# Row sums of the first six head pairs: two pairs per product group on four 32-column strips of TensorE, and all key-weight absolute values on VectorE

## The chip, the cores and the metric

The program runs on one core of one Trainium2 chip. The metric is the device time of one execution, in microseconds. The engines are TensorE (PE in the profile; its weight loads are PEld), VectorE (DVE), ScalarE (ACT), GpSimd (POOL) and SyncE (SP, which here only issues DMAs).

## What is computed

Soft-capped attention feeds an RWKV-like channel mix. Sizes: batch 8, 12 heads, 448 positions, head size 64, model width 768, inner width 1024.

```
scores = cap * tanh(scale * q @ k.T / cap)
attn   = exp(scores - max);  attn /= sum(attn) + 1e-09
x      = attn @ v                          # heads side by side: [8, 448, 768]
xk, xr = mixes of x with the x of the position before (mu_k, mu_r)
k      = relu(xk @ w_k);  v = k * k @ w_v;  r = sigmoid(xr @ w_r)
out    = r * v
```

w_k, w_v and w_r arrive as 64-bit floats, in two 32-bit words, and are rebuilt on the chip.

## The kernel before, in words

The work goes by **pairs of heads**: 48 pairs, six per batch entry. A pair's exponentials stand transposed, keys on partitions. The 448 keys make three groups of 128 and 64 left over; the left keys of two pairs (an even one and the one behind it) share one tile, `p_left`, with one pair's on partitions 0 to 63 and the other's on 64 to 127.

A program that is written out in **steps** sets the order on every engine: each step runs through a list of operation names (`START_EVEN` and `START_ODD` for steps 0 to 13, lines 77 to 83) and emits each operation's instructions. Every engine works through its own queue strictly in that order. In `step` (line 794) the dictionary `pair` says how far behind the step an operation's pair is: S, tanh and exp work on pair i in step i, V (`values`) on pair i-1, and `sum_recip`, `norm`, `mix_old`, `mix_new` on pair i-2. VL (`values_left`) and L (`scores_left`) stand in even steps only and serve two pairs each.

The operations that matter here, one by one:

- **S0, S1, S2** (`scores`, line 267): two products per key group, one per head, f32, into a PSUM tile `s`. **L** (line 278): four products of 64 rows and 64 columns, the left keys of two pairs. All these use the pool `ps_s`, which has **two** tiles: a score tile can be written when the `tanh` that reads the tile two before it is done.
- **tanh and exp** (lines 288, 294): each one ACT instruction of 128x896; the result is a tile `p`. In an even step ACT's list reads tanh0, exp0, tanh1, tanhL, expL, exp1, mix_old, tanh2, exp2; in an odd one tanh0, exp0, mix_old, tanh2, tanh1, exp1, exp2.
- **V** (line 303): six products of 64 columns, two heads side by side, into PSUM tile `pv`. **VL** (line 313): four products of 64x64 that add the left keys of two pairs.
- **O** (`ones`, line 324), for the pairs in `ONES`, 0 to 5, only: products of a constant 1/32 with the tiles `p`, whose output has the row sums 64 times over. A pair takes six products of 64 columns, two side by side. **OL** (`ones_left`, line 334): four of 64x64 for the left keys of two pairs. O stands in each step from 1 to 6 (pair i-1), OL at the head of steps 2, 4 and 6.
- **sum_recip** (line 343): on DVE, a transposing reduction of the sums, the guard `grd` added, a reciprocal and a transposition that spreads it. **norm** multiplies the values by it; **mix_old** (ACT, line 409) and **mix_new** (DVE, line 419) make the mixed row from it and free `pv`.
- For pairs 6 and on the sums are made by DVE reductions (`red`, line 354) and a round trip through DRAM.
- **K** (`kpart`, line 448): products of the key matrix, in fp32r, that begin in step 7. Their tiles come from the pool `ps_k`, also that of the row sums.
- **Weights**: `weight_load` brings a piece of 128x384; `weight_abs` (line 511) takes the absolute value of the upper words; five DVE instructions per piece follow, one per `f` (`fill`) or in `weight_rest`. Pieces 0 to 15 are of w_k. `DABS` (line 42) names the pieces whose absolute value is on DVE: 0 and 1; ACT does the others.

Of the kernel before, what the change touches and what calls it, by code (L numbers as in the profile page):

```python
# [9 lines left out]
F32 = mybir.dt.float32  # L10
F32R = mybir.dt.float32r
AF = mybir.ActivationFunctionType
ALU = mybir.AluOpType
# [3 lines left out]
B, H, S, D = 8, 12, 448, 64  # L17
NP = H // 2
DM = H * D
DF = 1024  # L20
NF = DF // 128
ND = DM // 128
# [3 lines left out]
P = 128  # L26
# [12 lines left out]
QA = QM + KL  # L39
NSTEP = NPAIR + 6  # L40
ONES = (0, 1, 2, 3, 4, 5)
DABS = (0, 1)
Q2 = 1
PS = 10
PACE = 0.85
# [23 lines left out]
HALF = (slice(0, 64), slice(64, 128))  # L69
NB = 2 * S // 32  # L70
# [3 lines left out]

START_EVEN = """more weight_load gather load_qk load_v weight_store load_vl OL f sum_recip weight_low weight_rest S0 K S1 V
VL L relu tanh0 exp0 tanh1 k_store tanhL expL qk_high weight_sum f recip norm f red0 f S2 K exp1 relu mix_old
qk_low redL mix_new red1 x_high x_low k_store tanh2 K O K relu exp2 k_store f red2 weight_abs rec_store
x_store rec_load"""  # L80
START_ODD = """load_qk weight_load gather load_v sum_recip f f norm f f K S0 tanh0 exp0 mix_old relu k_store O K S1 S2 tanh2
tanh1 relu exp1 k_store exp2 V f weight_low red0 recip mix_new weight_rest weight_sum x_high qk_high qk_low
x_low K K weight_abs relu red1 red2 k_store x_store rec_store weight_store more rec_load"""
UNIT = """gather f f recip load_v.0 weight_load S0.0 S1.0 S2.0 V.0 V.1 S0.1 S1.1 S2.1 VL L tanh1.0 tanh0.0 exp0.0
# [9 lines left out]
def order(i):  # L94
    ops = LAST if i == NPAIR else UNIT if SW <= i <= NPAIR + 1 else START_ODD if i % 2 else START_EVEN
    if i == 8:
        ops = ops.replace("tanh2 K O K relu exp2", "K O K relu tanh2 exp2")
# [15 lines left out]
class Body:  # L113
# [209 lines left out]

    def ones(self, i):

        if i not in self.SUM:
            self.SUM[i] = self.ps_k.tile([P, 512], F32, name="kps")
        for g in range(3):
            ph = self.P32[i, g]
            for h, p in enumerate(HALF):  # L330
                self.nc.tensor.matmul(self.SUM[i][p, 0:S], self.one, ph[:, h, :],  # L331
                                      start=(i % 2 == 0 and g == 0), stop=(i % 2 == 1 and g == 2))

    def ones_left(self, i):

        ph = self.P32[i, "L"]
        self.SUM[i + 1] = self.ps_k.tile([P, 512], F32, name="kps")
        for p in range(2):
            for h, o in enumerate(HALF):
                self.nc.tensor.matmul(self.SUM[i + p][o, 0:S], self.one[HALF[p]], ph[HALF[p], h, :],  # L340
                                      start=(p == 1), stop=(p == 0))

    def sum_recip(self, i):

        nc = self.nc
        t = self.up.tile([P, NB // 2], F32, name="se", bufs=1)
        nc.vector.tensor_reduce(out=t, in_=self.SUM.pop(i)[:, 0:S].rearrange("p (b k) -> p b k", k=32),
                                axis=mybir.AxisListType.X, op=ALU.add, apply_transpose=True)
        nc.vector.tensor_scalar(t, t, self.grd, None, op0=ALU.add)
        nc.vector.reciprocal(t, t)  # L350
        r = self.R[i] = self.up.tile([P, 2, S], F32, name="r", bufs=1)[:, 0]
        nc.vector.transpose(out=r, in_=t.unsqueeze(2).to_broadcast([P, NB // 2, 32]))
# [441 lines left out]
    def step(self, i):  # L794

        even, unit = i % 2 == 0, SW <= i <= NPAIR + 1
        if unit and not even:
            return
        if self.maxima and even and i < NPAIR:
            self.row_maxima(i)  # L800
            self.row_maxima(i + 1)
        pair = dict(load_qk=i + 3, qk_high=i + 2, qk_low=i + 2, load_v=i, S=i, tanh=i, exp=i, red=i, load_vl=i, L=i)
        pair.update(dict.fromkeys("V gather recip rec_store rec_load".split(), i - 1))
        pair.update(O=i - 1, OL=i - 2)
        pair.update(dict.fromkeys("sum_recip norm mix_old mix_new x_high x_low x_store VL".split(), i - 2))
        name = dict(S="scores", V="values", VL="values_left", L="scores_left", O="ones", OL="ones_left")
        late = "gather recip rec_store rec_load red".split()
        first = "O OL sum_recip".split()
        two = "gather recip rec_store rec_load".split()
        nk = 0  # L810
        if unit:
            pair.update(VL=i - 2)
        seen = {}
        for op in order(i):
            g, j1 = (), 0
            if len(op) == 2 and op[0] in "lpdcs":
                self.tail_work(op)
                continue
            if "." in op:
                op, j1 = op[:-2], int(op[-1])  # L820
            if op[-1] in "012L" and op not in ("L", "VL", "OL"):
                op, g = op[:-1], (op[-1] if op[-1] == "L" else int(op[-1]),)
            if op in pair:
                j = pair[op] + j1
                if unit and op == "V":
                    j -= 1
                    if j < SW - 1:
                        continue
                if op in two:
                    if unit:  # L830
                        if j - 1 < NPAIR:
                            getattr(self, op + "_two")(j - 1)
                        continue
                    if j >= SW - 2:
                        continue
                if op == "load_qk" and i == 0 and Q2:
                    self.load_qk(2)
                if 0 <= j < NPAIR and op not in (late if j in ONES else first) and not (uncut(j) and op in ('qk_high', 'qk_low')):
                    getattr(self, name.get(op, op))(j, *g)
            elif op == "next":  # L840
                self.open_first()
            elif op == "K":
                self.kpart(*self.ksplit.pop((i, nk), (0, 0)))
                nk += 1
            elif op == "f":
                if i <= NPAIR:
                    self.fill()
            elif op == "weight_load":
                self.weight_load(i + seen.get(op, 0))
                seen[op] = 1  # L850
            elif op == "more":
                for _ in range(MORE.count(i)):
                    self.weight_load(i)
# [204 lines left out]
```

## Time and profile before

| | us |
|---|---|
| median of 3 runs | 895.08 (894.81 to 895.83) |
| the profiled execution's own time | 895.82 |
| its span, first to last instruction | 894.0 |
| PE busy | 881.2 (99%) |
| DVE busy | 734.8 (82%) |
| ACT busy | 623.1 (70%) |
| POOL busy | 415.0 (46%) |

The page gives busy time per engine, the span in 40 slices, and groups of instructions. The mean granted clock of TensorE is 0.998 of 2.4 GHz. Matmuls overlap in the records, and an f32 product appears as two MATMUL records, so the pace of PE is read from the distance between the starts of neighbours, not from a record's duration. In the timeline a record's fields are its start, its length with equal neighbours merged, engine, line, operation, output and inputs, shapes, count, and, in brackets, the engine's idle time before it and what ended that.

### The profile page before, as it was taken

The numbers are of one execution on the slowest core, as the hardware profiler recorded it, in microseconds if no ns is written. First come the engines' busy times: TensorE is split into PE (matmuls) and PEld (weight loads), VectorE is DVE, ScalarE is ACT, GpSimd is POOL, SyncE is SP. The second block draws the span as 40 slices with busy tenths as digits, with TensorE's granted clock in tenths as the row PEclk, the third lists the DMA queues.
The fourth block names the chain that finished last, engine by engine and source line by source line (L and its number), as shares of the span: only waits on it lengthen the run. The fifth ranks groups of instructions, "written<-read, shape, count | busy, mean of one in ns | idle before, by whom it ended". The sixth has DMA issues, their size and how long they took to land.

```text
span 894.0 us, 14329 instructions
## 1 busy us (share of the span) xinstructions
PE 881.2 (99%) x5046; PEld 694.7 (78%) x5046; DVE 734.8 (82%) x1115; ACT 623.1 (70%) x962; POOL 415.0 (46%) x399
## 2 busy tenths in 40 slices
PE   7999999999999999999999999999999999999997
PEld 2335556767766677777676999999999999999996
DVE  5868996888987887897886789888888888888883
ACT  7898878888887787787876776655545555555451
POOL 2343354555566585676774003444345434443440
PEclk9999999999999999999999999999999999999999
DMA  7354655766656776677647963233233322332301
GB/s 261 118 167 144 207 185 163 227 193 192 193 184 193 210 224 214 201 216 243 200 148 247 330 237 95 76 110 118 79 114 110 118 87 85 119 110 83 119 28 49
DMA packets 97562, 142.97 MB, mean 160 GB/s; under 512 B 11592, under 2 KB 86984, under 8 KB 96840
## 3 DMA queue, kind: packets, MB, share of 16 engines
q1 hardware_dynamic: 89704, 129.56, 46.3%
q10 hardware_dynamic: 7776, 12.39, 3.7%
q8 instruction: 42, 0.69, 0.3%
q14 instruction: 40, 0.33, 0.1%
HBM read 94.18 MB, written 45.33 MB: 156 GB/s over the span
## 4 chain that ended last, share of the span: by engine, by line
PE 94%; ACT 3%; DVE 1%; DMA 1%; issue 0%; SPq 0%; DVEq 0%; ACTq 0%
PE kps L469 26%; PE ps2a L720 22%; PE pv L310 12%; PE ps2c L720 11%; PE s L275 11%; PE ps2b L720 5%; PE pv L319 2%; PE s L285 2%; PE kps L331 1%; ACT p L291 1%; ACT p L301 1%; DMA sq<-r 0%; DVE ro L708 0%; PE kps L340 0%; DMA w<-wk 0%
## 5 line engine op out<-in xcount | busy, mean ns | idle before, releaser
L291 ACT ACTIVATE p<-s,scl_t 128x896 f32<-128x896 f32 x144 | 139.4, 997 | 17.0 <-PE s L275 11.3
L301 ACT ACTIVATE p<-p,cap_t 128x896 f32<-128x896 f32 x144 | 145.2, 1036 | 1.9
L469 PE MATMUL kps<-xkh,wkl 128*128 128x448 f32 x384 | 143.5, 374 | 0.1
L469 PE MATMUL kps<-xkl,wkh 128*128 128x448 f32 x384 | 140.7, 366 | 0.0
L356 DVE TRANSPOSE_TENSOR_REDUCE r<-p 128x28 f32<-128x896 f32 x126 | 136.0, 1092 | 5.7 <-ACT p L301 5.4
L469 PE MATMUL kps<-xkh,wkh 128*128 128x448 f32 x384 | 140.3, 365 | 0.0
L310 PE MATMUL pv<-p,rv 128*64 128x448 f32 x576 | 115.1, 544 | 0.0
L469 PEld LDWEIGHTS kps<-xkh,wkl 128*128 128x128 f32 x384 | 72.1, 188 | 25.7 <-issue 12.3
L310 PEld LDWEIGHTS pv<-p,rv 128*64 128x64 f32 x576 | 38.6, 136 | 66.5 <-issue 57.4
L469 PEld LDWEIGHTS kps<-xkl,wkh 128*128 128x128 f32 x384 | 72.1, 188 | 8.0 <-issue 2.8
L469 PEld LDWEIGHTS kps<-xkh,wkh 128*128 128x128 f32 x384 | 72.1, 188 | 5.8
L708 DVE TENSOR_TENSOR ro<-t,ro 128x384 fp32r<-128x384 f32 x70 | 52.8, 756 | 23.2 <-ACT ro L131 23.2
L137 POOL TENSOR_TENSOR qkl<-rqk,qkh 128x832 fp32r<-128x832 f32 x34 | 67.6, 1988 | 2.7
L708 DVE TENSOR_TENSOR vo<-x,vo 128x512 fp32r<-128x512 f32 x63 | 56.3, 902 | 11.3 <-ACT vo L131 11.0
L407 DVE TENSOR_TENSOR x<-pv,r 128x448 f32<-128x448 f32 x48 | 28.1, 618 | 45.3 <-DMA r<-rec_d 43.6
L554 POOL TENSOR_TENSOR wsq<-wa,wsq 128x384 f32<-128x384 f32 x24 | 25.9, 1080 | 84.4 <-DVE wsq L545 84.4
L752 ACT ACTIVATE rs<-rs 128x384 f32<-128x384 f32 x28 | 14.7, 525 | 65.1 <-DVE rs L725 65.1
L131 ACT CAST ro<-t 128x384 fp32r<-128x384 f32 x70 | 34.3, 509 | 30.5 <-POOL t L137 30.2
L137 POOL TENSOR_TENSOR xkl<-xk,xkh 128x448 fp32r<-128x448 f32 x46 | 53.0, 1152 | 3.8
L672 DVE SCALAR_TENSOR_TENSOR t<-xc,mu_r,t 128x256 f32<-128x256 f32 (+3 forms) x120 | 53.7, 500 | 0.8
L137 POOL TENSOR_TENSOR s<-s,t 128x384 f32<-128x384 f32 x13 | 13.6, 1048 | 75.0 <-DVE ro L708 75.0
L131 ACT CAST vo<-x 128x512 fp32r<-128x512 f32 x63 | 38.9, 618 | 10.3 <-POOL x L137 6.0
(209 smaller groups left out, 2386.3 us busy)
## 6 DMA issues: line engine op xcount, KB each, us to landing
rqk<-qk SPq DMA_DIRECT2D x47, 448.0 KB
k_d<-ko ACTq DMA_DIRECT2D x54, 224.0 KB
x_d<-x SPq DMA_DIRECT2D x48, 224.5 KB
out<-cp SPq DMA_DIRECT2D x56, 192.0 KB
rv<-v SPq DMA_DIRECT2D x48, 192.0 KB
r<-rec_d SPq DMA_DIRECT2D x36, 224.0 KB
kr<-k_d SPq DMA_DIRECT2D x7, 1024.0 KB
x<-k_d SPq DMA_DIRECT2D x7, 1024.0 KB
```

The costliest lines, as they stand in the source:

```text
L131: self.nc.scalar.copy(out, x)
L137: {"p": self.nc.gpsimd, "v": self.nc.vector}[e].tensor_sub(*a)
L275: nc.tensor.matmul(s[:, h, 0:S], qk[a][p, k], qk[b][p, 0:S], start=(n == 0), stop=(n == len(terms) - 1))
L291: self.nc.scalar.activation(p32, self.S.pop((i, g))[:, :, 0:S], AF.Tanh, scale=self.scl_t)
L301: self.nc.scalar.activation(p32, p32, AF.Exp, scale=1.0 if self.maxima else self.cap_t)
L310: nc.tensor.matmul(pv[p, 0:S], v[:, g, h, :], ph[:, h, :], start=(g == 0), stop=False)
L356: self.nc.vector.tensor_reduce(out=r1[:, :, 3 if g == "L" else g], in_=self.P32[i, g].rearrange("p h (b k) -> p (h b) k", k=32), axis=mybi ...
L407: self.nc.vector.tensor_mul(self.X[i % 2][:, 1:], self.PV[i][:, 0:S], self.R.pop(i))
L469: nc.tensor.matmul(self.kps[fc][:, 0:S], w, m[:, dc, :], start=first, stop=last)
L672: nc.vector.scalar_tensor_tensor(out=td, in0=self.XC[:, d, j0 + o + 1:j1 + o + 1], scalar=self.mu["r"][:, d:d + 1], in1=td, op0=ALU.mult, ...
L708: self.nc.vector.tensor_sub(lo, a, f(hi))
L720: self.nc.tensor.matmul(o, a[:, g], self.WS[p, g][w][:, m], start=first and part == 0 and g == 0, stop=last and part == 2 and g == KG[p] - ...
```

## The change

The row sums of two pairs are now made together, in even steps only. `ones` takes an even pair i: for each key group g and for the left keys it issues four products whose stationary operand has 32 columns, one per pair p and head h, into four strips of 32 PSUM partitions. `ones_left` is gone. O moves out of the odd steps and stands, in steps 2, 4 and 6, behind VL and ahead of L; `sum_recip` of an even pair moves from the head of the step to behind `weight_sum`. It reduces once for both pairs (`se`, kept for the odd step), and adds the guard with four small instructions per pair that also move 32 partitions each. `DABS` is now all 16 pieces of w_k.

```diff
-DABS = (0, 1)
+DABS = range(ND * DF // 384)
...
-START_EVEN = """more weight_load gather load_qk load_v weight_store load_vl OL f sum_recip weight_low weight_rest S0 K S1 V
-VL L relu tanh0 exp0 tanh1 k_store tanhL expL qk_high weight_sum f recip norm f red0 f S2 K exp1 relu mix_old
-qk_low redL mix_new red1 x_high x_low k_store tanh2 K O K relu exp2 k_store f red2 weight_abs rec_store
+START_EVEN = """more weight_load gather load_qk load_v weight_store load_vl f weight_low weight_rest S0 K S1 V
+VL O L relu tanh0 exp0 tanh1 k_store tanhL expL qk_high weight_sum f sum_recip recip norm f red0 f S2 K exp1 relu mix_old
+qk_low redL mix_new red1 x_high x_low k_store tanh2 K K relu exp2 k_store f red2 weight_abs rec_store
...
-START_ODD = """load_qk weight_load gather load_v sum_recip f f norm f f K S0 tanh0 exp0 mix_old relu k_store O K S1 S2 tanh2
+START_ODD = """load_qk weight_load gather load_v sum_recip f f norm f f K S0 tanh0 exp0 mix_old relu k_store K S1 S2 tanh2
...
-        if i not in self.SUM:
-            self.SUM[i] = self.ps_k.tile([P, 512], F32, name="kps")
-        for g in range(3):
-            ph = self.P32[i, g]
-            for h, p in enumerate(HALF):
-                self.nc.tensor.matmul(self.SUM[i][p, 0:S], self.one, ph[:, h, :],
-                                      start=(i % 2 == 0 and g == 0), stop=(i % 2 == 1 and g == 2))
-
-    def ones_left(self, i):
...
+        self.SUM[i] = self.ps_k.tile([P, 512], F32, name="kps")
+        for g in (0, 1, 2, "L"):
+            for q in range(4):
+                p, h = divmod(q, 2)
+                rows = HALF[p] if g == "L" else slice(0, P)
+                ph = self.P32[i if g == "L" else i + p, g]
+                self.nc.tensor.matmul(self.SUM[i][32 * q:32 * q + 32, 0:S], self.one[rows, 0:32], ph[rows, h, :],
+                                      start=(g == 0), stop=(g == "L"))
...
-        t = self.up.tile([P, NB // 2], F32, name="se", bufs=1)
-        nc.vector.tensor_reduce(out=t, in_=self.SUM.pop(i)[:, 0:S].rearrange("p (b k) -> p b k", k=32),
-                                axis=mybir.AxisListType.X, op=ALU.add, apply_transpose=True)
-        nc.vector.tensor_scalar(t, t, self.grd, None, op0=ALU.add)
+        if i % 2 == 0:
+            self.se = self.up.tile([P, NB // 2], F32, name="se", bufs=1)
+            nc.vector.tensor_reduce(out=self.se, in_=self.SUM.pop(i)[:, 0:S].rearrange("p (b k) -> p b k", k=32),
+                                    axis=mybir.AxisListType.X, op=ALU.add, apply_transpose=True)
+        t = self.up.tile([P, NB // 2], F32, name="st", bufs=1)
+        for q in range(4):
+            a = 32 * (2 * (i % 2) + q // 2)
+            nc.vector.tensor_scalar(t[32 * q:32 * q + 32], self.se[a:a + 32], self.grd[a:a + 32], None, op0=ALU.add)
...
-        pair.update(O=i - 1, OL=i - 2)
+        pair.update(O=i - 2)
```

**PE's queue, from the end of step 5 to L of step 6.** Line numbers of the two programs differ by a few; L310 is V, L319 VL, L285 L, L340 the old OL, L332 the new O, L275 the scores. Before, from S1 and S2 of step 5:

```order
L275 MATMUL s<-rqk 128x448 x4
L310 MATMUL pv<-p_521,rv 64x448 x2
L310 MATMUL pv<-p_524,rv 64x448 x2
L310 MATMUL pv<-p_541,rv 64x448 x2
L340 MATMUL kps<-p_left,one 64x448 x4
L275 MATMUL s<-rqk 128x448 x4
L310 MATMUL pv<-p_575,rv 64x448 x2
L310 MATMUL pv<-p_594,rv 64x448 x2
L310 MATMUL pv<-p_592,rv 64x448 x2
L319 MATMUL pv<-p_left,rvl 64x448 x4
L285 MATMUL s<-rqk 64x448 x4
```

The change, from V of pair 5 in step 6 to L:

```order
L310 MATMUL pv<-p_585,rv 64x448 x2
L310 MATMUL pv<-p_597,rv 64x448 x2
L310 MATMUL pv<-p_595,rv 64x448 x2
L319 MATMUL pv<-p_left,rvl 64x448 x4
L332 MATMUL kps<-p_525,one 32x448 x2
L332 MATMUL kps<-p_585,one 32x448 x2
L332 MATMUL kps<-p_528,one 32x448 x2
L332 MATMUL kps<-p_597,one 32x448 x2
L332 MATMUL kps<-p_555,one 32x448 x2
L332 MATMUL kps<-p_595,one 32x448 x2
L332 MATMUL kps<-p_left,one 32x448 x4
L285 MATMUL s<-rqk 64x448 x4
```

Sixteen products for the sums of pairs 4 and 5 now stand between VL and L, where nothing stood.

**PE's queue, from L of step 4 on.** Before:

```order
L285 MATMUL s<-rqk 64x448 x4
L275 MATMUL s<-rqk 128x448 x2
L331 MATMUL kps<-p_421,one 64x448 x2
L331 MATMUL kps<-p_440,one 64x448 x2
L331 MATMUL kps<-p_438,one 64x448 x2
L275 MATMUL s<-rqk 128x448 x2
L331 MATMUL kps<-p_521,one 64x448 x2
L331 MATMUL kps<-p_524,one 64x448 x2
L331 MATMUL kps<-p_541,one 64x448 x2
L275 MATMUL s<-rqk 128x448 x4
```

The change, up to V of pair 4:

```order
L285 MATMUL s<-rqk 64x448 x4
L275 MATMUL s<-rqk 128x448 x8
L310 MATMUL pv<-p_525,rv 64x448 x2
L310 MATMUL pv<-p_528,rv 64x448 x2
L310 MATMUL pv<-p_555,rv 64x448 x2
```

S2 of step 4 and S0, S1, S2 of step 5 (eight products) now follow each other with nothing between.

**DVE's queue, steps 4 and 5.** L407 and L403 are norm, L422 and L418 mix_new, L537 and L533 the first instruction of a piece of weights, L511 its absolute value. Before:

```order
L407 TENSOR_TENSOR x_151<-pv,r 128x448
L422 SCALAR_TENSOR_TENSOR xk<-x_151,mu_k,pv 128x448
L347 TENSOR_REDUCE se<-kps 128x14
L349 TENSOR_SCALAR se<-se,grd 128x14
L350 RECIPROCAL se<-se 128x14
L352 STREAM_TRANSPOSE r<-se 128x448
L537 TENSOR_SCALAR wt<-wsq 128x384
L539 TENSOR_SCALAR wa<-wt 128x384
L407 TENSOR_TENSOR x_153<-pv,r 128x448
```

The change:

```order
L340 TENSOR_REDUCE se<-kps 128x14
L345 TENSOR_SCALAR st<-se,grd 32x14 x4
L346 RECIPROCAL st<-st 128x14
L348 STREAM_TRANSPOSE r<-st 128x448
L403 TENSOR_TENSOR x_151<-pv,r 128x448
L418 SCALAR_TENSOR_TENSOR xk<-x_151,mu_k,pv 128x448
L511 TENSOR_SCALAR wsq<-w_469 128x384
L345 TENSOR_SCALAR st<-se,grd 32x14 x4
L346 RECIPROCAL st<-st 128x14
L348 STREAM_TRANSPOSE r<-st 128x448
L533 TENSOR_SCALAR wt<-wsq 128x384
L535 TENSOR_SCALAR wa<-wt 128x384
```

The even pair's reduction stands right ahead of its norm; the odd pair's has gone; an absolute value has come in behind mix_new.

## Rows read from the trace of the kernel before

**Rows 1.** Busy time by stretch: start:end, length, then busy us per engine.

```profile
43.58:61.09 17.51, 17.51 (x98) 5.77 (x100) 12.18 (x28) 15.49 (x18) 6.87 (x9) 1.00 0.48 151
79.00:97.00 18.00, 17.92 (x90) 10.16 (x82) 14.73 (x28) 15.39 (x20) 5.49 (x8) 1.00 0.62 193
```

**Rows 2.** Timeline of PE, L of step 4 to L of step 6.

```profile
42.58 0.93 PE L285 MATMUL s<-rqk 64*64 64x448 f32 x8
43.44 1.02 PE L275 MATMUL s<-rqk 64*128 64x448 f32 x4
44.40 2.48 PE L331 MATMUL kps<-p,one 128*64 128x448 f32 x12
...
54.27 0.98 PE L340 MATMUL kps<-p_left,one 64*64 64x448 f32 x8
55.18 1.77 PE L275 MATMUL s<-rqk 64*128 64x448 f32 x8
56.89 2.48 PE L310 MATMUL pv<-p,rv 128*64 128x448 f32 x12
59.29 0.98 PE L319 MATMUL pv<-p_left,rvl 64*64 64x448 f32 x8
60.09 0.93 PE L285 MATMUL s<-rqk 64*64 64x448 f32 x8
```

**Rows 3.** Timeline of ACT, tanhL of step 4 to tanhL of step 6.

```profile
43.58 1.01 ACT L291 ACTIVATE p_left<-s,scl_t 128x896 f32<-128x896 f32 x1 [1.48 <-PE s L285]
...
49.03 0.55 ACT L517 ACTIVATE wsq<-w 128x384 f32<-128x384 f32 x1
49.49 0.99 ACT L291 ACTIVATE p<-s,scl_t 128x896 f32<-128x896 f32 x1
...
52.02 1.88 ACT L291 ACTIVATE p<-s,scl_t 128x896 f32<-128x896 f32 x2
...
61.09 1.01 ACT L291 ACTIVATE p_left<-s,scl_t 128x896 f32<-128x896 f32 x1 [1.86 <-PE s L285]
```

**Rows 4.** Waits of PE, first 160 us: us in total, times, longest.

```profile
PE s L285 <- ACT p L291: 0.8, 1, 0.8
```

**Rows 5.** Timeline of ACT, step 1.

```profile
14.01 0.54 ACT L517 ACTIVATE wsq<-w 128x384 f32<-128x384 f32 x1
14.46 0.99 ACT L291 ACTIVATE p<-s,scl_t 128x896 f32<-128x896 f32 x1
...
16.88 1.91 ACT L291 ACTIVATE p<-s,scl_t 128x896 f32<-128x896 f32 x2 [0.35 <-PE s L275]
```

**Rows 6.** Timeline of PE, steps 0 to 2.

```profile
3.99 3.36 PE L275 MATMUL s<-rqk 64*128 64x448 f32 x8 [3.99 <-DMA rqk<-qk]
...
14.16 0.97 PE L331 MATMUL kps<-p,one 128*64 128x448 f32 x4 [0.99 <-ACT p L301]
...
25.00 0.93 PE L285 MATMUL s<-rqk 64*64 64x448 f32 x8
```

**Rows 7.** Timeline of DVE: an absolute value, and sum_recip of step 6.

```profile
9.84 0.36 DVE L515 TENSOR_SCALAR wsq<-w 128x384 uint32<-128x384 uint32 x1 [1.85 <-DMA w<-wk]
...
56.66 0.64 DVE L347 TRANSPOSE_TENSOR_REDUCE se<-kps 128x14 f32<-128x448 f32 x1
57.34 0.23 DVE L349 TENSOR_SCALAR se<-se,grd 128x14 f32<-128x14 f32 x1
```

**Rows 8.** Timeline of ACT, step 7.

```profile
70.75 0.64 ACT L417 ACTIVATE pv<-x,om_k 128x448 f32<-128x448 f32 x1 [1.69 <-DVE x L407]
71.32 1.89 ACT L291 ACTIVATE p<-s,scl_t 128x896 f32<-128x896 f32 x2
```

**Rows 9.** Timeline of PE, step 8: K between S0 and S1, then L.

```profile
73.97 0.47 PE L469 MATMUL kps<-xkh,wkl 128*128 128x448 f32 x1
...
75.40 1.02 PE L275 MATMUL s<-rqk 64*128 64x448 f32 x4
...
79.56 0.93 PE L285 MATMUL s<-rqk 64*64 64x448 f32 x8
```

More of the change, by code (lines that the diff above doesn't have):

```diff
@@ L96, in order @@
     if i == 8:
-        ops = ops.replace("tanh2 K O K relu exp2", "K O K relu tanh2 exp2")
+        ops = ops.replace("tanh2 K K relu exp2", "K K relu tanh2 exp2")
     if i == SW:
@@ L324, in ones @@
     def ones(self, i):
-        if i not in self.SUM:
-            self.SUM[i] = self.ps_k.tile([P, 512], F32, name="kps")
-        for g in range(3):
-            ph = self.P32[i, g]
-            for h, p in enumerate(HALF):
-                self.nc.tensor.matmul(self.SUM[i][p, 0:S], self.one, ph[:, h, :],
-                                      start=(i % 2 == 0 and g == 0), stop=(i % 2 == 1 and g == 2))
-    def ones_left(self, i):
[L336 to L341, printed above, removed]
+        self.SUM[i] = self.ps_k.tile([P, 512], F32, name="kps")
[6 more added lines that the diff above has]
+                                      start=(g == 0), stop=(g == "L"))
     def sum_recip(self, i):
         nc = self.nc
-        t = self.up.tile([P, NB // 2], F32, name="se", bufs=1)
-        nc.vector.tensor_reduce(out=t, in_=self.SUM.pop(i)[:, 0:S].rearrange("p (b k) -> p b k", k=32),
-                                axis=mybir.AxisListType.X, op=ALU.add, apply_transpose=True)
-        nc.vector.tensor_scalar(t, t, self.grd, None, op0=ALU.add)
+        if i % 2 == 0:
[6 more added lines that the diff above has]
+            nc.vector.tensor_scalar(t[32 * q:32 * q + 32], self.se[a:a + 32], self.grd[a:a + 32], None, op0=ALU.add)
         nc.vector.reciprocal(t, t)
@@ L803, in step @@
         pair.update(dict.fromkeys("V gather recip rec_store rec_load".split(), i - 1))
-        pair.update(O=i - 1, OL=i - 2)
+        pair.update(O=i - 2)
         pair.update(dict.fromkeys("sum_recip norm mix_old mix_new x_high x_low x_store VL".split(), i - 2))
-        name = dict(S="scores", V="values", VL="values_left", L="scores_left", O="ones", OL="ones_left")
+        name = dict(S="scores", V="values", VL="values_left", L="scores_left", O="ones")
         late = "gather recip rec_store rec_load red".split()
-        first = "O OL sum_recip".split()
+        first = "O sum_recip".split()
         two = "gather recip rec_store rec_load".split()
@@ L820, in step @@
                 op, j1 = op[:-2], int(op[-1])
-            if op[-1] in "012L" and op not in ("L", "VL", "OL"):
+            if op[-1] in "012L" and op not in ("L", "VL"):
                 op, g = op[:-1], (op[-1] if op[-1] == "L" else int(op[-1]),)
```

## The prediction

> **What bounds the kernel now.** The change touches the first eight of the program's steps, so I read that stretch alone, first by busy time, then PE's timeline of one period (two steps), then ACT's over the same period. Between L of step 4 and L of step 6 PE is busy for all of 17.51 us, ACT for 15.49, DVE for 12.18 [rows 1]. A busy PE could still be waiting inside its records, so the starts matter: 42.58, 43.44, 44.40 and so on to 60.09 follow each other at the pace of the work [rows 2], and ACT sits idle before tanhL for 1.48 and 1.86 us until PE's L is done [rows 3]. So PE is the bound here, and a period is the sum of PE's work: 60.09 - 42.58 = 17.51 us. From step 8 on PE is as dense (17.92 of 18.00 [rows 1]). What is lost or won up to there reaches the end of the program unless later work waits for something else.
>
> The reader should see one more thing in these rows: the row sums of odd steps stand between score products that would otherwise have to wait. A score tile is free only when the tanh two tiles earlier is done. PE never shows that wait here, because the sums fill the time until then; it shows it once in 160 us, for 0.8 us [rows 4].
>
> **What O costs, before and after.** Before, V's six products (three slots of two 64-column strips) take 56.89 to 59.29 = 2.40 us [rows 2]. A pair's O has the same shape and the same 2.48 us record; I take 2.40 for it too. OL takes 54.27 to 55.18 = 0.91. Two pairs: 2 x 2.40 + 0.91 = 5.71 us. After: sixteen products in four slots of four strips. No operation here has four streams over the same 128 rows, so I bound it. If four strips take what two take, the three key groups cost V's 2.40 and the left keys what VL or OL cost (0.80 or 0.91): 3.25. If only two strips run at once, it is 2 x 2.40 + 0.91 = 5.7. I take 3.25, because the nearest row, OL, already runs four products at once, in 64x64 corners, in the time of one slot. Cheaper than 3.2 it can hardly be: each product still streams 448 columns at the pace of V's. PE's own work in a period becomes 17.51 - 5.71 + 3.25 = 15.05 us.
>
> The Trainium skill ("TensorE: Matmul & The Clock Gate", Part 3, "Measured speedup vs the span model") gives 2.38 times for three 32-column tiles, 0.79 of the ideal. By that, an estimate, the three groups would cost 2.40 / 0.79 = 3.0 us and the end would come 1.9 us later than I forecast. No run here shows it yet.
>
> **Where O moves to is the point.** It leaves the odd step, where PE would wait for score tiles anyway, and stands behind V and VL and ahead of L, and tanhL is what ACT waits for. I follow the longest chain of a period.
>
> - L to tanhL: 42.58 to 43.58 = 1.00 [rows 2, 3].
> - ACT from tanhL of step 4 to the end of tanh1 of step 5: 43.58 to 52.02 + 1.88 = 53.90, that is 10.32 us [rows 3]. One absolute value in it goes: 49.03 to 49.49 = 0.46. Left: 9.86.
> - Only then is the tile free that S0 of step 6 writes. PE from there: S0 and S1 1.71 (55.18 to 56.89), V 2.40, VL 0.80 [rows 2], O 3.25: 8.16 us to the start of L.
>
> Sum: 1.00 + 9.86 + 8.16 = 19.0 us against 17.51: **+1.5 us a period**. PE is idle for 19.0 - 15.0 = 4.0 us of it. ACT has in the second part only exp1, exp2 and the next three instructions, and then waits for L some 4 us, where it waited 1.86. The point from which the period is longer than before is O = 17.51 - 1.00 - 9.86 - 4.91 = 1.74 us; O is about 3.
>
> The period up to L of step 2: tanh0 of step 1 starts 0.45 earlier (the absolute value at 14.01 goes) and ends at 15.00 [rows 5]; S2 of step 1 takes 0.96 (as 43.44 to 44.40) and V of pair 0 2.40: PE is at 18.36. tanh1 is done by then (16.88 + 1.91 - 0.45 - 0.35 = 17.99 [rows 5]). With 8.16 more L starts at 26.5, against 25.00 [rows 6]: +1.5. The periods ending in steps 4 and 6 give +1.5 each.
>
> Steps 7 and 8: PE loses O of pair 5, 2.40 us, but ACT there waits 1.69 us for norm on DVE and starts the last two tanh at 71.32, done at 73.21 [rows 8], 13.12 us after L of step 6. Ahead of that norm DVE loses a reduction (0.64), and gains an absolute value (0.36) and three small additions (0.23 each at most) [rows 7]: between -0.3 and +0.4, I take 0. Then S0 0.95, K 1.43 (73.97 to 75.40 [rows 9]), S1 0.95, V and VL 3.20: L of step 8 is 19.7 us after L of step 6, before it was 79.56 - 60.09 = 19.47 [rows 2, 9]. So **+0.2**, and the 2.40 us are not given back.
>
> **What I cost at nothing.** Fourteen absolute values go from ACT to DVE, 14 x 0.36 = 5.0 us [rows 7]. DVE has 17.51 - 12.18 = 5.3 us idle in a period [rows 1], and two or three of them fall in one. The guard's four small instructions replace one; per two pairs six more at 0.23, less a reduction of 0.64: +0.7. The same idle time hides it. Without that cover it would be late in one place: absolute value, additions, reciprocal and transposition stand between mix_new of the even pair and norm of the odd one, and mix_old, inside ACT's chain, waits for that norm. That is 0 to 0.4 us a period, up to +1.2 in all, kept for the range. sum_recip of the even pair now waits on DVE until O is done, with norm and mix_new behind it; ACT wants its result only after tanhL, expL and exp1, some 3 us after L, and reduction to norm takes about 2.5, begun 0.9 before L's end. SP's DMAs keep their order; a weight load can wait a little longer for its buffer, and nothing needs these weights before step 7.
>
> **Sum.** 3 x 1.5 + 0.2 = +4.7 us. On the profiled execution, 895.82, that is 900.5. The median of the runs lies 0.74 below it, so I predict 895.08 + 4.7 = **899.8**. The case's own range: step 8 could give 1.7 back if norm there is no longer late (898.1), and the waits on DVE could add 1.2, a slower O 1 to 2: 898 to 902.5.
>
> **The rivals.**
>
> *PE's saved time comes through (faster).* PE is busy throughout, so 3 x (5.71 - 3.25) = 7.4 us less work would give 887.7. For it: PE's 17.51 of 17.51, and ACT being relieved at the same time. Against it: it needs the chain above to be under 15.0 us, 4 us shorter than the rows say, that is, score tiles free well before the tanh that reads them ends. It decides wherever ACT plus PE's tail stays under PE's own work. Chance 0.11.
>
> *Loss and gain nearly cancel.* Half the waits I count, and step 8 giving its 1.7 back: +0.5, about 895.6. Chance 0.07.
>
> *The strips run only two at once*, so the change does not do what its shape says. O at 5.7 makes each of three tails 2.45 longer: 899.8 + 7.4 = 907.2. For it: four streams would read twice as much per partition as anything in this trace. Against it: OL. Chance 0.13.
>
> *The clock falls.* The first score products, after 3.99 us of idling, took 3.36 us for eight records [rows 6], where step 6's took 1.77 [rows 2]: the lower level, 1.2 GHz, against 2.4. After 0.99 us of idling nothing fell: four records in 0.97 [rows 6]. The new 4.0 us of idling a period lie between, split over two places with products between. If the clock fell there, V behind them would double, 2.4 us a period, and S1 and S2 with it, 4.1: 907 to 912. The Trainium skill ("TensorE: Matmul & The Clock Gate", "Why this matters for your kernels") advises against such idle gaps between bursts of matmuls. The trace agrees for the first gap and shows nothing of the kind for the short one. Chance 0.05.
>
> **How the numbers follow.** The forecast has 0.64. A measurement of this kernel can tell about 0.2% (1.8 us) from no change; the forecast and the two slow rivals are slower than that, together 0.82; cancelling is 0.07, faster 0.11. The range 897.0 to 907.5 takes in the forecast with its bounds and the two-strip case, and leaves out the faster and cancelling cases and most of the clock's.
>
> **What would show it.** Right: starts of L of steps 2, 4 and 6 near 26.5, 45.5 and 64.5 (before 25.00, 42.58, 60.09); PE waiting for a tanh ahead of S1, S2 and the next S0; ACT waiting some 4 us before tanhL; the four slots of O in 3.2 us; no PE waits from step 8 on that were not there. Wrong: L of step 6 at or before 60; a long wait of ACT for norm; O over 4 us; products of V stretched to twice their pace.

## The result, and the profile after

The changed kernel takes **907.40 us** (median of 4 runs, 905.88 to 908.73). The kernel before, run beside it, takes 895.42 (894.81 to 895.83). The ratio is 1.0136 [1.0121, 1.0151]: slower by 12.0 us. The forecast was 899.8, in a range of 897.0 to 907.5: slower, as forecast, and by two and a half times as much as the forecast 4.7. The profiled execution is the shortest of the four, 905.88 with a span of 904.1, 10.06 us above the profiled 895.82 of before. The accounts below are made on these two; the other 1.9 us of the 12.0 lie between executions of which there is no trace.

From the page, busy time per engine:

```profile
PE 879.9 (97%) x5046; PEld 693.0 (77%) x5046; DVE 747.7 (83%) x1144; ACT 617.3 (68%) x948; POOL 415.7 (46%) x399
```

PE does little less in all, and no longer all the time. Where the time goes is in the timeline of PE, from O of step 2 to L of step 8:

```profile
23.42 2.46 PE L332 MATMUL kps<-p,one 128*32 128x448 f32 x24
25.81 0.96 PE L332 MATMUL kps<-p_left,one 64*32 64x448 f32 x8
26.70 0.98 PE L285 MATMUL s<-rqk 64*64 64x448 f32 x8
...
32.26 1.02 PE L275 MATMUL s<-rqk 64*128 64x448 f32 x4 [2.44 <-ACT p L291]
34.23 1.86 PE L275 MATMUL s<-rqk 64*128 64x448 f32 x4 [0.95 <-ACT p L291]
36.03 3.09 PE L310 MATMUL pv<-p,rv 128*64 128x448 f32 x12
39.05 1.77 PE L275 MATMUL s<-rqk 64*128 64x448 f32 x8
...
47.35 0.98 PE L285 MATMUL s<-rqk 64*64 64x448 f32 x8
...
52.98 1.02 PE L275 MATMUL s<-rqk 64*128 64x448 f32 x4 [2.50 <-ACT p L291]
54.95 1.87 PE L275 MATMUL s<-rqk 64*128 64x448 f32 x4 [0.95 <-ACT p L291]
56.75 4.67 PE L310 MATMUL pv<-p,rv 128*64 128x448 f32 x12
61.34 1.77 PE L275 MATMUL s<-rqk 64*128 64x448 f32 x8
...
69.64 0.98 PE L285 MATMUL s<-rqk 64*64 64x448 f32 x8
...
89.13 0.93 PE L285 MATMUL s<-rqk 64*64 64x448 f32 x8
```

Three things are to be seen, beside [rows 2]. O takes 23.42 to 26.70 = 3.28 us. The score products of the odd steps wait for tanh, 2.44 and 0.95 us, where O used to fill the time. And behind these waits PE is slow: V of pair 4 takes 4.67 us for the work that took 2.48, S2 ahead of it 1.87 for 1.02. The view by stretch says why. Its columns are those of [rows 1]: PE, PEld, DVE, ACT and POOL busy, then the granted clock. The stretches run from L to L:

```profile
26.70:47.35 20.65, 17.09 (x101) 5.07 (x97) 18.58 (x38) 14.68 (x16) 7.30 (x9) 0.92 0.40 127
47.35:69.64 22.29, 18.67 (x100) 5.35 (x96) 15.70 (x32) 14.86 (x16) 8.54 (x10) 0.85 0.39 119
69.64:89.13 19.49, 17.51 (x89) 7.55 (x89) 18.83 (x39) 14.69 (x16) 5.71 (x8) 1.00 0.37 114
```

The granted clock is 0.92 and 0.85 where it was 1.00: part of each stretch ran at 1.2 GHz. DVE is busy for 18.58 us of the first (13.75 before, from L to L) and for 15.70 of the second (12.18 before). The timeline of ACT shows where that is felt:

```profile
27.75 1.01 ACT L291 ACTIVATE p_left<-s,scl_t 128x896 f32<-128x896 f32 x1 [4.86 <-PE s L285]
36.83 0.64 ACT L413 ACTIVATE pv<-x,om_k 128x448 f32<-128x448 f32 x1 [1.57 <-DVE x L403]
37.41 1.88 ACT L291 ACTIVATE p<-s,scl_t 128x896 f32<-128x896 f32 x2
...
48.40 1.01 ACT L291 ACTIVATE p_left<-s,scl_t 128x896 f32<-128x896 f32 x1 [4.23 <-PE s L285]
57.19 0.64 ACT L413 ACTIVATE pv<-x,om_k 128x448 f32<-128x448 f32 x1 [1.22 <-DVE x L403]
57.77 1.89 ACT L291 ACTIVATE p<-s,scl_t 128x896 f32<-128x896 f32 x2
```

ACT waits some 4 to 5 us for L, as forecast, and in the middle of its chain, ahead of mix_old, 1.57 and 1.22 us for norm on DVE. Before, ACT came to mix_old and to the two tanh behind it ([rows 3], 52.02) without such a wait:

```profile
51.46 0.62 ACT L417 ACTIVATE pv<-x,om_k 128x448 f32<-128x448 f32 x1
```

| | before | after | gain or loss | forecast |
|---|---|---|---|---|
| start of L of step 2 | 25.00 | 26.70 | +1.70 | +1.5 |
| L of step 2 to L of step 4 | 17.58 | 20.65 | +3.07 | +1.5 |
| step 4 to step 6 | 17.51 | 22.29 | +4.78 | +1.5 |
| step 6 to step 8 | 19.47 | 19.49 | +0.02 | +0.2 |
| the rest | | | +0.5 | 0 |

### The profile page after: what moved, and what is told of

Its sections match the earlier page's. It is cut to its first block, busy times and chain, and to the rows that moved or that the text cites. A ratio compares the mean times of both kernels' runs of the same rounds, so it can differ in the third digit from the quotient of the medians.

```text
span 904.1 us, 14301 instructions
## 1 busy us (share of the span) xinstructions
PE 879.9 (97%) x5046; PEld 693.0 (77%) x5046; DVE 747.7 (83%) x1144; ACT 617.3 (68%) x948; POOL 415.7 (46%) x399
## 4 chain that ended last, share of the span: by engine, by line
PE 92%; ACT 3%; DVE 3%; DMA 1%; issue 0%; SPq 0%; DVEq 0%; ACTq 0%
PE kps L465 26%; PE ps2a L716 22%; PE pv L310 12%; PE ps2c L716 11%; PE s L275 10%; PE ps2b L716 5%; PE pv L319 2%; PE s L285 2%; ACT p L291 1%; PE kps L332 1%; ACT p L301 1%; DVE r L352 1%; DMA sq<-r 0%; ACT p_left L301 0%; DVE ro L704 0%
## 5 line engine op out<-in xcount | busy, mean ns | idle before, releaser
L310 PE MATMUL pv<-p,rv 128*64 128x448 f32 x576 | 117.9, 555 | 0.0
L310 PEld LDWEIGHTS pv<-p,rv 128*64 128x64 f32 x576 | 39.2, 139 | 69.3 <-issue 57.2
L403 DVE TENSOR_TENSOR x<-pv,r 128x448 f32<-128x448 f32 x48 | 28.2, 619 | 38.8 <-DMA r<-rec_d 38.7
L275 PE MATMUL s<-rqk 64*128 64x448 f32 x168 | 44.5, 626 | 15.9 <-ACT p L291 11.6
L475 ACT ACTIVATE ko<-kps 128x448 f32<-128x448 f32 x64 | 32.3, 539 | 24.5 <-PE kps L465 17.3
```

The costliest lines, as they stand in the source:

```text
L275: nc.tensor.matmul(s[:, h, 0:S], qk[a][p, k], qk[b][p, 0:S], start=(n == 0), stop=(n == len(terms) - 1))
L310: nc.tensor.matmul(pv[p, 0:S], v[:, g, h, :], ph[:, h, :], start=(g == 0), stop=False)
L475: self.nc.scalar.activation(ko, ps[:, 0:S], AF.Relu)
```

## The experiments

The theories: **A**, what costs time is the place of O in the tail between VL and L (the forecast's chain); **B**, it is the fourteen absolute values on DVE; **C**, products of 32 columns are themselves slow; **D**, DVE is late with the sums whatever the place of O. These letters are the text's; in an expectation a letter means what its own bracket says. Each job ran the kernel before beside it; its median lay between 895.4 and 896.7.

**1. The absolute values alone**, in the kernel before:

```diff
-DABS = (0, 1)
+DABS = range(ND * DF // 384)
```

> The kernel before with one edit: the absolute values of all 16 key-weight pieces on VectorE. Theory A (the loss is the new place of the row sums, made worse by late norms and by a lower TensorE clock after its new idle gaps): PE stays dense up to step 8, so the time is that of before within 1.5 us, 894 to 897. Rival B (VectorE is overloaded by the absolute values, and that is most of the 12 us): 900 or more.

Measured: 896.25 (895.66 to 898.44) against 895.59, ratio 1.001 [1.0001, 1.002]. L of steps 2, 4, 6 at 24.98, 42.49, 60.01, as before; ACT waits 0.85 and 0.94 us for norm, and PE's own work hides it. B falls as the sole cause.

**2. The sums alone**: the changed kernel with the old `DABS`.

```diff
-DABS = range(ND * DF // 384)
+DABS = (0, 1)
```

> The changed kernel with one edit: absolute values of pieces 2 to 15 back on ScalarE, so only the row sums differ from before. Theory A: L of step 6 still starts 7 to 10 us later than the 60.09 of before, time 904 to 908. Rival B: most of the loss goes, 895 to 900.

Measured: 909.15 (907.04 to 910.58), ratio 1.0157 [1.0135, 1.0178], more than expected; L of step 6 starts at 72.94, 12.85 us late. The loss comes with the sums. With ACT's work longer, its waits for norm are 0.22 and 0.72, but the V at the end of the odd steps ran slow in all three places, by the timeline of PE:

```profile
17.08 3.35 PE L310 MATMUL pv<-p,rv 128*64 128x448 f32 x12
...
38.87 4.40 PE L310 MATMUL pv<-p,rv 128*64 128x448 f32 x12
...
61.27 3.44 PE L310 MATMUL pv<-p,rv 128*64 128x448 f32 x12
```

**3. PE kept busy**: the changed kernel with eight products in each of steps 3 and 5 whose result nobody reads, where O used to stand.

```diff
+    def busy(self):
...
+        for h, p in enumerate(HALF):
+            self.nc.tensor.matmul(self.filler[1][p, 0:S], self.one, self.P32[i - 1, 0][:, h, :], start=True, stop=True)
...
-mix_old relu k_store K S1 S2 tanh2
+mix_old relu k_store busy busy busy K S1 busy S2 tanh2
```

> The changed kernel with work added: in steps 3 and 5 TensorE does six extra products of 64 columns (result unused) ahead of S1 and two ahead of S2, where it idled 2.4 to 2.5 and 0.95 us. Theory A, clock part: V of pairs 2 and 4, 3.1 and 4.7 us in the changed kernel, takes 2.5 in both; S0 of steps 4 and 6 then waits for its tanh instead; L of step 6 starts about 3 us earlier than 69.64, time 902 to 904, although TensorE does more. Rival C (the clock loss is hidden behind other waits): time as the changed kernel's, 905.9 to 908.7, or up to 1 us more.

Measured: 905.77 (905.3 to 912.01), ratio 1.0142 [1.0104, 1.018]: less gain than expected. V of pairs 2 and 4 is back at 2.48 us. V of pair 0, in step 1, where nothing was added, is not (first line):

```profile
16.55 3.08 PE L311 MATMUL pv<-p,rv 128*64 128x448 f32 x12
...
36.35 2.48 PE L311 MATMUL pv<-p,rv 128*64 128x448 f32 x12
39.61 1.92 PE L276 MATMUL s<-rqk 64*128 64x448 f32 x8 [0.78 <-ACT p L292]
...
57.26 2.48 PE L311 MATMUL pv<-p,rv 128*64 128x448 f32 x12
60.36 1.92 PE L276 MATMUL s<-rqk 64*128 64x448 f32 x8 [0.63 <-ACT p L292]
```

L of step 2 to L of step 6 takes 40.95 us instead of 42.94, although PE does more. But the score products behind V now wait for tanh, since ACT waits 1.57 and 1.42 for norm: under the low clock lay the next wait.

**4. norm ahead of the weights on DVE**, in odd steps (lines of the order lists, cut at their ends):

```diff
-load_qk weight_load gather load_v sum_recip f f norm f f K
+load_qk gather load_v sum_recip norm weight_abs weight_load f f f f K
-k_store f red2 weight_abs rec_store
+k_store f red2 rec_store
```

> The changed kernel with norm of the odd pair moved up on VectorE: the absolute values and the first two instructions of a weight piece come behind it, not ahead (the weight load of odd steps is issued behind them too). Theory A: ScalarE's wait for norm in steps 3 and 5 falls from 1.57 and 1.22 us to under 0.6, but S0 of steps 4 and 6 then still waits for the V that runs at the lower clock, so the time falls by under 1.5 us against the changed kernel, 905 to 908. Rival D (the wait for norm is what lengthens the chain): 2.5 to 3.5 us less, 903 to 905.

Measured: 908.85 (906.99 to 909.22), ratio 1.0148 [1.0131, 1.0165]. The waits for norm fall to 0.58 and 0.66; V of pairs 2 and 4 takes 3.32 and 4.71 us, and nothing is won. Taking away the one loss without the other shows the other.

**5. Both edits**, with the filler of run 3 in step 1 too.

```diff
-        if i not in (3, 5):
+        if i not in (1, 3, 5):
```

> The two edits of e3 and e4 together, and TensorE kept busy in step 1 too (extra products, result unused). Theory A (clock and late norm hide each other, each alone gives little): V of pairs 0, 2 and 4 takes 2.5 us, the wait for norm stays under 0.7 us, a period from L to L takes 19.2 us, L of step 6 starts at 65 (changed kernel 69.64, before 60.09), time 900 to 902: what is left is the price of the order alone, near the 4.7 us that were forecast. Rival C (neither matters): 905 or more.

Measured: 905.85 (903.52 to 907.3), ratio 1.0096 [1.0067, 1.0126]: missed, 900 to 902 was expected. The clock and the odd pairs' norms are in order, the periods are not:

```profile
26.73:46.33 19.60, 19.02 (x116) 5.56 (x112) 17.55 (x35) 14.69 (x16) 7.86 (x10) 1.00 0.44 135
46.33:67.34 21.01, 19.11 (x116) 5.57 (x112) 17.51 (x35) 14.79 (x16) 8.54 (x10) 1.00 0.40 126
```

In the second one ACT waited for the even pair's norm. O ended at 46.33, but DVE, at the weights without a pause, began to reduce its sums only at 48.03:

```profile
48.03 0.64 DVE L351 TRANSPOSE_TENSOR_REDUCE se<-kps 128x14 f32<-128x448 f32 x1
...
51.75 0.64 ACT L424 ACTIVATE pv<-x,om_k 128x448 f32<-128x448 f32 x1 [1.35 <-DVE x L414]
```

**6. O behind S2 of the even step**, out of the tail; norm of the even pair goes to the end of the even step, mix_old and mix_new to the odd step, where the odd pair's norm follows them, and `p_left` gets two buffers (parts of the order):

```diff
-VL O L relu
+VL L relu
-S2 K exp1 relu mix_old
+S2 O K exp1 relu
```

> The changed kernel with the same sixteen 32-column products and the same absolute values on VectorE, but the products placed behind S2 of the even step, where TensorE idled, not between VL and L; the even pair's norm, mix_old and mix_new follow later (its mixing in the odd step), and p_left has two buffers. Theory A (the place is the loss): ScalarE waits under 2 us for L, the clock stays up, a period takes 17 to 18 us, L of step 6 starts at 59 to 62, time 893 to 898, that of before or a little less. Rival E (the four-strip products or the absolute values themselves cost): 903 or more.

Measured: 905.99 (905.23 to 909.31), ratio 1.0109 [1.0077, 1.0141]: missed by 8 us. ACT waits less for L (1.42, 2.67, 2.67), but V now waits for a free `pv`, and two of these V ran slow:

```profile
33.26 4.17 PE L319 MATMUL pv<-p,rv 128*64 128x448 f32 x12 [1.68 <-DVE xk L427]
...
53.46 4.17 PE L319 MATMUL pv<-p,rv 128*64 128x448 f32 x12 [2.05 <-DVE xk L427]
```

The sums now come at the end of O, 28.43, and DVE waits for them:

```profile
28.57 0.65 DVE L349 TRANSPOSE_TENSOR_REDUCE se<-kps 128x14 f32<-128x448 f32 x1 [3.63 <-PE kps L341]
```

mix_new of the even pair, which frees its `pv`, ends at 33.21, just ahead of the first V above. Two tiles `pv` do not bridge that time.

**7. The place alone**: `DABS` as before, the filler in steps 1, 3 and 5, DVE's order as in the change.

```diff
-DABS = range(ND * DF // 384)
+DABS = (0, 1)
-        if i not in (3, 5):
+        if i not in (1, 3, 5):
```

> The changed kernel with DABS back at (0, 1) and with the unused products in steps 1, 3 and 5 that keep PE's clock up: what is left of the change is the new place of O and the late sums. Theory A (O in the tail between VL and L costs about 1.5 to 2 us in each of three places, absolute values on ACT costing 0.46 of it again): V of pairs 0, 2 and 4 in 2.48 us, L of step 6 at 66 to 67, ACT's waits for norm under 0.7 us in steps 3 and 5, the time 901 to 903. Theory B (the sums come so late that DVE holds ACT anyway, whoever makes the absolute values): waits for norm stay over 1 us, L of step 6 at 68 or later, the time 905 or more.

Measured: 905.19 (903.07 to 907.78), ratio 1.0082 [1.0056, 1.0109]; above the 901 to 903 of the expectation's A, while the long waits of its B did not come (0.18 and 0.72). Three of the six executions took 903.1 to 903.6; the profiled one is the longest, 907.78.

```profile
28.91:49.02 20.11, 18.95 (x117) 5.66 (x113) 17.95 (x35) 16.06 (x19) 7.17 (x8) 1.00 0.44 132
49.02:68.89 19.87, 19.09 (x116) 5.56 (x112) 13.66 (x30) 15.66 (x18) 8.25 (x10) 1.00 0.44 133
```

At full clock, and with hardly a wait for norm, a period takes 20.11 and 19.87 us. ACT made two absolute values in the first period's chain (0.91 us, 35.41 to 36.32) and one in the second (0.46). Without them it is, by subtraction, about 19.2 and 19.4, against the forecast's 19.0. The even pair's norm does not hold ACT here: with the absolute values back on ACT, DVE is busy for 13.66 us of the second period, for 17.51 in run 5. The rest of the profiled miss lies ahead: L of step 2 came at 28.91, since the score products from 9.37 on ran at the low clock here (eight records in 3.36 us).

**8. A shorter O**: run 5 with key groups 1 and 2 left out of O.

```diff
-for g in (0, 1, 2, "L"):
+for g in (0, "L"):
```

> The run with the clock held and norm ahead, in which O leaves out key groups 1 and 2 (so the row sums of the first six pairs lack those keys): O is two slots of four strips, about 1.65 us, in place of 3.28. Theory A (O's length in the tail is paid in full, and the sums come as much earlier): each of the three tails is 1.6 us shorter than in that run, L of steps 2, 4 and 6 at 25.1, 43.1 and 62.5 (there 26.73, 46.33, 67.34), the time 901, about what the forecast's break-even of 1.74 us for O says plus what is lost in steps 8 to 10. Theory B (O's length is covered by ACT's or DVE's work, which sets the period): periods within 0.5 us of that run's 19.60 and 21.01, the time 904 or more.

Measured: 903.41 (902.5 to 906.49), ratio 1.0075 [1.0044, 1.0106].

```profile
25.67:43.76 18.09, 17.52 (x100) 5.04 (x97) 16.04 (x34) 14.69 (x16) 6.58 (x9) 1.00 0.47 145
43.76:64.96 21.20, 17.60 (x100) 5.04 (x96) 19.21 (x36) 14.80 (x16) 8.74 (x11) 1.00 0.41 125
```

With O at 1.78 us (23.89 to 25.67) the first period is 1.5 shorter than in run 5, as the expectation's A says. The second is not: there ACT waited 3.05 us, at 50.88, for the even pair's norm, on a DVE that was busy for 19.21 of 21.20 us: O ended at 43.76, and the reduction of its sums began at 46.96. So A holds in the one period, D in the other.

**9. Four strips for one pair, in the old place**: groups 0 and 1 side by side, then group 2 and the left keys, in the kernel before; no OL, five small additions per pair on DVE in place of one, and two buffers for `p_left`.

```diff
+        for n, g in enumerate((0, 1, 2, "L")):
+            rows = HALF[i % 2] if g == "L" else slice(0, P)
+            for h in range(2):
+                q = 2 * (n % 2) + h
+                self.nc.tensor.matmul(self.SUM[i][32 * q:32 * q + 32, 0:S], self.one[rows, 0:32], ph[rows, h, :],
+                                      start=(n < 2), stop=(n > 1))
```

> The kernel before with O left where it was, once per pair, but with four strips of 32 columns used for one pair: groups 0 and 1 side by side, then group 2 and the left keys, so two slots a pair, 3.2 us for two pairs in place of 5.71, and no OL; five small additions on DVE a pair join the two halves. Theory A (what cost time was O's place in the tail, not the four strips): the chain L to tanhL 1.00, ACT 10.32, S0 to VL 4.91 sets the period, 16.2 us in place of 17.51, so 3 to 4 us faster than before, 891 to 893, as far as ACT does not wait for norm longer than now; the four additions more on DVE could take 1 us a period of it back, and the new idle of PE, about 1.2 us a period, should not bring the clock down. Theory C (32-column strips or the small additions themselves cost the time): as before or slower, 895 to 899.

Measured: 900.73 (898.64 to 901.72), ratio 1.0036 [1.0018, 1.0053]: slower, not faster. Up to L of step 4 hardly anything was won (42.34 for 42.58), for O of a pair did not come down to the 1.6 us expected:

```profile
26.79 1.70 PE L332 MATMUL kps<-p,one 128*32 128x448 f32 x12
28.41 0.94 PE L332 MATMUL kps<-p_left,one 64*32 64x448 f32 x4
29.29 1.02 PE L275 MATMUL s<-rqk 64*128 64x448 f32 x4
```

That is 2.50 us (before, 2.40 and half of OL's 0.91): group 2's products of 128 rows and the left keys' of 64 did not run at once. In the next period ACT waited 1.72 us for norm, PE then 2.19 for ACT, and the granted clock of the period was 0.85.

**10. The same with all products over 128 rows**: the left keys' stationary operand is zero on the other pair's half.

```diff
+            one = self.half[:, i % 2] if g == "L" else self.one[:, 0:32]
```

> The once-per-pair run with one thing changed: the left keys' products also take all 128 rows, with a stationary operand that is zero on the other pair's half. In that run a pair's O took 2.48 us (26.79 to 29.27), three slots: group 2's products of 128 rows and the left keys' of 64 rows stood side by side in the order but did not run at once. Theory A (products run at once when their rows are the same, and then the sums cost two slots): O of a pair takes 1.65 us; the chain of 16.2 us a period then shows, where ACT does not wait for norm: L of steps 2 and 4 at 24.2 and 41, the time 2 to 3 us under that run's 900.73 unless PE's new idle brings the clock down as it did there from 50.76 on (22.33 us for that period); then no better than it. Theory C (four strips run as two pairs of two here): O stays at 2.4 us and nothing changes.

Measured: 899.61 (898.45 to 901.88), ratio 1.0028 [1.001, 1.0046]. O of a pair now takes 25.53 to 27.17 = 1.64 us:

```profile
25.53 1.32 PE L336 MATMUL kps<-p,one 128*32 128x448 f32 x10
...
27.17 1.02 PE L279 MATMUL s<-rqk 64*128 64x448 f32 x4
```

And the period shows it once, 16.68 us for 17.58; in the next one ACT waits 2.40 us for norm, PE 3.58 for ACT, and the granted clock is 0.85:

```profile
23.72:40.40 16.68, 15.45 (x100) 4.68 (x96) 15.30 (x33) 15.11 (x20) 6.50 (x9) 1.00 0.49 158
40.40:62.44 22.04, 18.37 (x101) 5.50 (x97) 16.87 (x43) 16.72 (x20) 8.30 (x10) 0.85 0.38 120
```

**11. That and norm ahead of the weights** in steps 1 to 7, in even steps too (parts of the order).

```diff
-load_vl f sum_recip weight_low weight_rest S0
+load_vl sum_recip S0
-recip norm f red0 f S2
+recip norm weight_low weight_rest f f red0 f f S2
-load_qk weight_load gather load_v sum_recip f f norm f f K
+load_qk gather load_v sum_recip norm weight_load f f f f K
```

> The same, with norm ahead of the weights' instructions on DVE in steps 1 to 7. Theory A (a new wait of ACT for norm, 1.72 us at 48.07 in the once-per-pair run, made PE idle 2.19 us and the clock fall): no wait for norm over 0.7 us in steps 2 to 6, V of all pairs in 2.48 us, periods of 16.3 to 16.8 us, L of step 6 at 58 (before 60.09), the time 892 to 895, lower than the other's. Theory D (DVE is late with or without this order, since the additions and the weights fill it): waits for norm stay over 1 us or V waits for the mixed row, periods at 17.5 or more, 896 or more.

Measured: 898.48 (896.98 to 903.36), ratio 1.0017 [0.9992, 1.0041]: not told apart from the kernel before, and short of A's 892 to 895. In step 5 ACT waits 3.17 us for norm all the same. The timelines of DVE and of POOL there:

```profile
48.34 0.23 DVE L350 TENSOR_SCALAR su<-se,grd 64x14 f32<-64x14 f32 x1
48.61 2.58 DVE L354 TENSOR_TENSOR st<-se,su 32x14 f32<-32x14 f32 x4
```

```profile
48.48 1.14 POOL L141 TENSOR_TENSOR xkl<-xk,xkh 128x448 fp32r<-128x448 f32 x1
49.57 1.00 POOL L559 TENSOR_TENSOR wsq<-wa,wsq 128x384 f32<-128x384 f32 x1
```

Four additions of 32x14 that take 0.17 us each where POOL is idle (run 10, at 60.18) took 2.58 together, beside POOL's work.

**12. Only pairs 0 to 3 so**, pairs 4 and 5 and steps 6 and on as in the kernel before.

```diff
+        if i > 3:
+            return self.ones_two(i)
```

> The last run's program for pairs 0 to 3 and steps 0 to 5 only; pairs 4 and 5 have the sums of the kernel before (two strips, six products and the left keys apart), and steps 6 and on its order. In that run L of step 4 came 1.9 us before that of the kernel before, and the lead went in the period behind it, where ACT waited 3.17 us at 52.84 for a norm, four additions on DVE having taken 2.58 us. Theory A (two slots a pair in the old place save time wherever DVE is in time): L of step 4 at 40.7, and the lead of 1.9 us stays behind it, the time 893.2 to 895, 1 to 3 us under the kernel before. Theory D (DVE is late in step 5 all the same, since pair 3's sums fall there): the norm of pair 3 waits over 2 us, the lead is lost by step 6 and the time is 895 to 898.

Measured: 897.46 (896.66 to 898.04), ratio 1.0016 [1.0003, 1.003]. D's case: L of steps 2 and 4 comes at 24.17 and 41.21, 0.8 and 1.4 us ahead, then pair 3's norm keeps ACT for 3.20 us, at 53.38, and the lead is gone by L of step 6 (60.06). Up to L of step 10 it falls 1.1 us behind (102.40 for 101.27), which no run explains. No version that was tried is faster than the kernel before.

## Why the prediction was right, and where it was wrong

The direction came for the reason given. Two terms that the sum put at nothing failed: the clock, set apart as a rival, and the wait for norm. The prediction had named both among its signs of being wrong, "a long wait of ACT for norm" and "products of V stretched to twice their pace".

**Right: the direction and the tail.** PE's saved 2.4 us a period did not come through, and for the reason given: O moved from a place where PE has to wait anyway into the tail that ACT waits for. PE's waits stand where they were forecast ahead of S1 and S2 of the odd step (2.44 and 0.95), though none stands ahead of the next S0, and ACT's wait for L is 4.86 and 4.23 us, "some 4". L of step 2 came at 26.70 for 26.5. The tail is paid in full where nothing else is late (run 8).

**Right by luck: the 19.0.** With the clock held and few waits for norm the period was the forecast's 19.0 to within 0.4, less ACT's absolute values (run 7). But the path was another. The forecast let S0 wait for the second of the last two tanh. It takes the tile that the first one frees: in the changed kernel it starts at 39.05, while the second ends at 39.29, and in run 3, where it waits, at 39.61, with the first done at 39.56. What holds S0 when nothing is late is S2 and V of the odd step, which begin only when tanh0 is done. In run 5's first period that leg, from tanhL at 27.78 to S0 at 37.63, is 9.85 us, by chance the 9.86 that was counted. The 907.2 of the two-strip rival, beside the measured 907.4, is chance too: O took 3.28 us, not 5.7.

**Right: O.** Four strips of 32 columns took the three key groups in 2.39 us (23.42 to 25.81), where two strips of 64 take 2.40 [rows 2]; with the left keys 3.28, forecast 3.25. The estimate of 3.0 us for the three groups, worked out from the Trainium skill's 2.38 times ("TensorE: Matmul & The Clock Gate", Part 3, "Measured speedup vs the span model"), did not come true: the measurement decides.

**Wrong, and the largest term: the clock.** The prediction set the fall of the clock apart, as a rival with a chance of 0.05, and gave the sum without it. It was a term of the sum. On the chain from L to L, where one tanh takes 0.99 us:

- Step 2 to 4: L to tanhL 1.05, ACT to the end of the tanh that frees the tile of S0 10.65 (37.41 plus 0.99 is 38.40), V at the low clock 0.65 longer than that, then S0 to L 8.30. Together 20.65.
- Step 4 to 6: 1.05, then 10.36 (to 58.76), then S2 and V at the low clock, 1.87 and 4.67 us, holding S0 back by 2.58, then 8.30. Together 22.29.

So the low clock shows with 0.65 + 2.58 = 3.2 us of the 5.4 by which the profiled loss (10.06) exceeds the forecast (4.7). The wait for norm, below, is 1.3; longer legs in the two periods make 0.4, L of step 2 makes 0.2, and the end behind step 8 adds 0.5; step 6 to 8 takes 0.2 off. I reasoned that 0.99 us of idling had been harmless and 3.99 not, and that the new gaps are split, with products between. They were 2.44 and 0.95 us, and the four records between them did not keep the clock up. The 3.99 us, too, were a poor measure: they stand ahead of the first product, so they show a clock that had not risen yet, not one that fell. The Trainium skill's advice against idle gaps, cited from the same page ("Why this matters for your kernels"), speaks of a single gap longer than either of these; the trace shows 1.2 GHz behind the two shorter ones. The gaps alone do not decide. In step 1 they are 1.83 and 0.95 us in the changed kernel, and V of pair 0 takes 2.48; in run 3, which has the same program there, they are 1.88 and 0.95, and it takes 3.08. That the median lies 1.5 us above the profiled execution fits this: the granted clock over the whole execution is 0.993 in the profiled one and 0.988 to 0.991 in the three others (0.998 before). It is not shown where they lost it, since only one has a trace.

**Wrong: "What I cost at nothing", the wait for norm.** I allowed 0 to 0.4 us a period and took 0. It was 1.57 and 1.22. Without the waits the chain has 9.08 and 9.14 us on ACT, for the 9.86 that I counted, because of the tile; so of the waits about 0.8 and 0.5 us show in the period. The error was to compare DVE's idle time in a period with the added work. DVE had the time, but not at that place: one or two absolute values, four additions, a reciprocal and a transposition stand between the even pair's mixed row and the odd pair's norm, and the four additions did not take 0.23 us each, as [rows 7] has it, but 1.75 and 1.95 together. Runs 1 and 2 show that neither part alone makes this wait cost much.

**The two hide each other.** Run 3 took the low clock away, and a wait for tanh came; run 4 took the waits away, and V at the low clock set the pace. That is why the losses must not be added from single experiments, and why run 5, with both edits, is still 9 us slower: what is left is the tail (19.6 for 17.6), the even pair's norm behind a busy DVE, and waits of V (0.78) and K (1.60) in step 8.

**Steps 6 to 10.** Step 6 to 8 is +0.02 (forecast 0.2), and that is two errors that cancel: norm was later (ACT waits 2.77 us for it, for 1.69 in [rows 8]), and S0 again needed only the first of the last two tanh. The late norm comes out one step on. DVE's norm is 10.23 us later than before in step 7 and 10.22 in step 8, L of step 8 only 9.57 (between the two norms lie DVE's reductions and the round trip through DRAM); behind this norm stand mix_old and then K, which waits for a tile that ACT should have emptied:

```profile
93.89 0.64 ACT L413 ACTIVATE pv<-x,om_k 128x448 f32<-128x448 f32 x1 [0.74 <-DVE x L403]
```

```profile
95.04 0.47 PE L465 MATMUL kps<-xkh,wkl 128*128 128x448 f32 x1 [0.79 <-ACT ko L475]
```

This is the 0.7 us that L of step 8 to L of step 10 adds. I had looked no further than L of step 8.

## What to carry to other kernels

Work that fills a wait can be free where it stands and paid in full where it goes to: before merging or shrinking products, look at which engine waits behind the new place. TensorE, given idle time, can lose its clock, and then the loss is in the work behind the gap, so a new gap belongs into the sum, as a term that may or may not come, and not among the rivals. And when the cover of small work is idle time, look for it at the place on the chain and not in the period's total. And a number that comes out says little before its path does: here 19.0 and 907.2 both met a measurement by chance.

## What the runs showed of the hardware that I had not expected

- **A small addition on DVE that began beside a POOL instruction mostly ended with it.** The changed kernel's additions take 0.22 us, but the one at 32.93 took 1.01 and ended at 33.94; POOL's instruction, begun at 32.77, ended at 33.91. In two periods the four additions took 1.75 and 1.95 us:

```profile
32.93 1.75 DVE L345 TENSOR_SCALAR st<-se,grd 32x14 f32<-32x14 f32 x4
```

```profile
32.77 1.14 POOL L137 TENSOR_TENSOR xkl<-xk,xkh 128x448 fp32r<-128x448 f32 x1
```

Those that kept their time with POOL busy lay at a gap between two of its instructions, as the one at 48.34 in run 11 (POOL ends at 48.40 and begins anew at 48.48). A reciprocal did not wait: before, the one at 31.11 took 0.24 us with POOL busy from 30.98 to 32.13. All this was read from the traces; no run was made for it.

- **Products of 128 and of 64 rows did not run side by side.** Two of 128 rows and two of 64 rows, in strips of their own, ran one pair after the other (2.50 us for a pair's sums, run 9); with 128 rows for all the same sums took 1.64 (run 10). Four of 64 rows do run at once, as OL (0.91 us for its four products [rows 2]).
